# Second-layer weights interleaved high and low, two operands moved to other byte offsets, and one load moved ahead, in a retention, experts and feed-forward kernel

## The chip, the cores and the metric

The kernel runs on one core of one Trainium2 chip. The metric is the time of one execution in microseconds of device time, as the median of several runs; lower is better. One more execution is recorded by the hardware profiler, and all rows below come from it.

## What is computed

Three layers follow each other. The first is a retention layer (8 batches, 8 heads, 576 positions, 64 channels). Its output, 4608 tokens of 512 channels, goes through 8 experts, one of which is chosen for each token. The last layer, which the change is mostly about, is a plain feed-forward layer with a squared ReLU:

```python
def _moe_ref(x, modality_id, w_gate, modality_bias, w1, w2):
    logits = x @ w_gate + modality_bias[modality_id]
    e_idx = np.argmax(logits, axis=1)
    ...
        h = np.maximum(x[mask] @ w1[e], 0.0)
        out[mask] = gate_w[mask, None] * (h @ w2[e])

def _moe2_ref(x, w_in, w_out):        # x 4608x512, w_in 512x2048, w_out 2048x512
    h = np.maximum(x @ w_in, 0.0)
    return (h * h @ w_out).astype(np.float32)
```

## The kernel before

Every product of the experts and of the last layer is made of three TensorE matmuls in the float32r type: each operand is held as a high part and a low part (the rest), and high times high, high times low and low times high are summed in PSUM.

**Experts (`phase12`).** Tokens are sorted by expert into slots "E" and 0 to 8, each of 8 blocks; `us` lists the blocks, numbered i. Blocks 56 to 63 are slot 6 (448 tokens wide), 64 to 71 slot 7 (384 wide), 72 to 79 slot 8 (256 wide). For block i, `first` of block i+1 (12 matmuls, then `hh` on ACT and `hl` on DVE), a transposition of the next slot's tokens where due (`xh` on ACT, `xl` on DVE), and `second` of block i (12 matmuls) are written down in this order. After them come the block's side tasks: splitting the next expert weights (`wx`, `wy`), a portion of the generator `cs`, which converts the last layer's weights (steps L745 to L768, then `cwh` on ACT and `cwl` on DVE, then a store to DRAM as `wc`), and steps of the generator `ex`, which is `combos`. The first step of `combos` first runs all that is left of `cs` (L798), and then issues the load of `eyr`, 1 MB, the first 512 tokens of the last layer's input (L802). Its further steps make the sums and differences that the last layer needs of them (`etx`, `x`).

**Last layer (`phase3`).** It works on 2x2 blocks with 7 products instead of 8, per tile of 512 tokens (9 tiles) and per 256 of the 2048 hidden channels (8 of these, in three passes of 3, 2 and 3, `PASSES`). `one` makes a first-layer product, with weights as the stationary and x as the moving operand; `two` a second-layer product, with h as the stationary and weights as the moving operand. `six` writes the six matmuls of either (L1199 to L1201): stationary high with moving high, stationary high with moving low, stationary low with moving high, twice. All are 128x128 by 256 columns. There are 3024 in the first layer and 3024 in the second. `Plan` sets the order of phase 3: each operation has a cost, what it reads and writes by key, and a due time counted back from TensorE, and the planner lays them out engine by engine. Its loads of weights are `loadw`, at the start of a pass; the loads ahead of the first pass are `wload2` in `phase12`. Loads and stores are issued by SP in the order written.

**Where operands lie.** An address counts bytes within a partition. In the built program before, every x and w tile of the last layer starts at a multiple of 128 (`w000` at 41088, `x0` at 49280, `w100` at 131200), and so do `xh`, `xl`, `hh`, `hl`, `wx` and `wy` of the experts. The three `h` tiles are the exception: they start at 147680, 162016 and 176352, which is 96 above a multiple of 128. All steps inside these tiles are multiples of 512 bytes. The high and low parts of a second-layer weight are two tiles, 8 to 32 KB apart.

Of the kernel before, what the change touches and what calls it, by code (L numbers as in the profile page):

```python
# [25 lines left out]
P = 128  # L26
# [66 lines left out]
def kernel(ctx, tc, qT, kT, kN, vN, modT, w_gate, mbias, w1, w2, w_in, w_out,  # L93
# [318 lines left out]
    def run(gen, n):  # L412
        for _ in range(n):
            if next(gen, 0) == 0:
                return False
        return True
# [298 lines left out]
    def phase12():  # L715
        ring[0] = psG
        with ExitStack() as c1:
# [285 lines left out]
            for i, u in enumerate(us):  # L1003
                s, f = u
                k = seq.index(s)
                nx = seq[k + 1] if k + 1 < len(seq) else None
                if nx is not None and f == (4 if s == "E" else 0):
                    gather(nx)
                if i + 1 < len(us):
                    first(us[i + 1])  # L1010
                if nx is not None:
                    if s == "E" and f == 6:
                        trans(nx, 0)
                        trans(nx, 1)
                    elif s != "E" and 3 <= f <= 6:
                        trans(nx, f - 3)
                if u == (NF, 7):
                    wload2(1, 0, wp)
                if i == 71:
                    tc.mark_branch_hint_location("extra0", 0, HINTED)  # L1020
                second(u)
                if s == "E" and f == 6:
                    trans(nx, 2)
                    trans(nx, 3)
                if i == 2:
                    route_c(last)
                if i == 0:
                    for _ in route_a(last):
                        pass
                    next(cs)  # L1030
                elif i == 1:
                    tb = table()
                    next(tb)
                    for _ in route_b(last, dve):
                        next(tb)
                elif i == 2:
                    ws(6, 2, 7)
                    tab_out()
                    turn = tab_turn()
                    next(turn)  # L1040
                    for _ in range(10):
                        next(tb)
                elif i == 3:
                    while next(tb) != "set":
                        pass
                    turn = chain(turn, tb)
                    ws(8, 2, 11)
                else:
                    wl(i + 9)
                    run(turn, 9)  # L1050
                    fill(wsg(i + 6, 2 if i < 10 else 1, i + 9), part(cs, 2250))
                    if i >= 65:
                        run(ex, 1 if i == 65 else 2)
                    if i == 73:
                        assert next(cs, 0) == 0 and next(ex, 0) == 0
                        extras()
                        wload2(0, 0, cv)
                if u == (NF, 1):
                    wload2(0, 1, wp)
                if u == (NF, 5):  # L1060
                    wload2(0, 2, wp)
                if i == 6:
                    ext = nc.values_load(slots[0:1, 3, 0:1], min_val=0, max_val=NX)
# [3 lines left out]

    def wload2(m, j, pool_, load=True):
        for x in range(2):
            held["w", m, j, x] = pool_.tile([P, 7, 256], F32R, tag="w", name=f"w{m}{j}{x}")  # L1070
            if load:
                sp.dma_start(held["w", m, j, x].bitcast(F32).rearrange("p m c -> p (m c)"), wc[m, PASSES[0][j], x])

# [73 lines left out]
    def phase3():  # L1147
        with ExitStack() as c2:
# [4 lines left out]
                wload2(1, j, wp, False)  # L1153
            WT = [[[held["w", m, j, x] for x in range(2)] for j in range(3)] for m in range(2)]
            XT = [held["x", m] for m in range(7)]
            HT = [sb(f"h{j}", [P, 2, 7, 256]) for j in range(3)]
            ZT = [sb(f"z{j}", [P, 8, 256], F32) for j in range(3)]
            yr = rp.tile([P, KD, TS], F32, tag="raw", name="yr")
            xt = sb("xt", [P, 2, 256], F32)
# [29 lines left out]
            def dma(o, i, kb, r, w, early=False):  # L1189
                plan.add(m_(kb), lambda e: (pool if early else e).dma_start(o, i), r, w, 2.0)  # L1190
# [15 lines left out]
            def loadw(p, m, j0=0):  # L1206
                for j, fp in list(enumerate(PASSES[p]))[j0:]:
                    for x in range(2):
                        dma(WT[m][j][x].bitcast(F32).rearrange("p m c -> p (m c)"), wc[m, fp, x], 917,
                            [], [("w", m, j, x)])  # L1210

# [101 lines left out]
            def two(n, x):  # L1313
# [4 lines left out]
                for q in range(len(PASSES[p])):  # L1318
                    u = HS_[n, q]
                    h, m, w, mo = HT[u % 3], MH[x], WT[1][q], MO[x]  # L1320
                    plan.add(MMS, six([ps[:, 0, :], ps[:, 1, :]],
                                      [((h[:, 0, m, P * b:P * b + P], h[:, 1, m, P * b:P * b + P]),
                                        (w[0][:, mo, :], w[1][:, mo, :])) for b in range(2)],
                                      x in (1, 2, 5) and q == 0),
                             [("h", u % 3, m, 0), ("h", u % 3, m, 1), ("w", 1, q, 0), ("w", 1, q, 1)], [kr])
                v = VO[n]
                oe = OE[v]
                o = {1: oe[:, 0:2, 256:512], 6: oe[:, 0:2, 0:256], 4: oe[:, 2:4, 256:512],
# [101 lines left out]
```

## Time and profile before

| | |
|---|---|
| median of 3 runs | 1345.21 us (1340.93 to 1346.01) |
| the profiled execution: its time | 1348.41 us |
| the profiled execution: span from first to last instruction | 1346.5 us |
| mean granted TensorE clock | 0.995 |
| TensorE (PE) busy | 1312.9 us, 98%, 10639 matmuls |
| weight loads of TensorE (PEld) busy | 1226.4 us, 91% |
| VectorE (DVE), ScalarE (ACT) busy | 76%, 46% |
| DMA, mean over the span | 246 GB/s |
| the last layer on TensorE | from 607.9 to 1338.9 us |

Matmuls are pipelined, so a busy PE says only that it seldom waits: each matmul of the last layer is shown as some 280 ns long, but a new one starts every 117 to 120 ns. What a matmul costs is read from the distance of starts in the order of time.

### The profile page before, as it was taken

The page shows a single profiled execution, that of the slowest core. Times are in us where ns is not written, and L with a number is a line of the kernel's source. Part 1 is how long each engine was busy: PE and PEld are TensorE (multiplying, and loading weights), DVE is VectorE, ACT ScalarE, POOL GpSimd, SP SyncE. Part 2 cuts the span into 40 slices and gives each one's busy share as a digit, 9 for nine tenths or more (in the row PEclk, how much of TensorE's full clock was granted, in tenths as well). Part 3 has the DMA queues.
Part 4 walks back from the last instruction along what each step waited for, and adds up shares of the span by engine and source line. Part 5 has one row for each costly group of instructions (what it writes and reads, how often), then busy time and mean ns, then how long its engine had stood idle before and what let it go on. Part 6 is the DMA issues. An engine that isn't in the chain of part 4 may idle for free.

```text
span 1346.5 us, 26963 instructions
## 1 busy us (share of the span) xinstructions
PE 1312.9 (98%) x10639; PEld 1226.4 (91%) x10639; DVE 1022.8 (76%) x2095; ACT 624.5 (46%) x1283; POOL 125.2 (9%) x170
## 2 busy tenths in 40 slices
PE   7999989999999999999999999999999999999997
PEld 7888877888888889899999999999999999999996
DVE  3787858878787788647788888758788777776665
ACT  1444344454545545536655666534434444433343
POOL 3222112101110110000000000000000011111121
PEclk9999989999999999999999999999999999999999
DMA  9998257788787877887554445668799755655551
GB/s 330 391 351 300 77 189 237 278 279 294 246 299 244 318 263 233 295 330 294 218 208 189 173 172 204 251 257 310 282 342 342 294 203 200 211 174 173 173 188 48
DMA packets 139957, 331.90 MB, mean 246 GB/s; under 512 B 15185, under 2 KB 52849, under 8 KB 139825
## 3 DMA queue, kind: packets, MB, share of 16 engines
q1 hardware_dynamic: 132208, 309.82, 64.3%
q0 software_dynamic: 5840, 19.14, 4.0%
q8 instruction: 85, 1.39, 0.4%
q10 hardware_dynamic: 1776, 1.17, 0.3%
q14 instruction: 48, 0.39, 0.1%
HBM read 222.33 MB, written 107.78 MB: 245 GB/s over the span
## 4 chain that ended last, share of the span: by engine, by line
PE 50%; DVE 4%; ACT 1%; issue 0%; POOL 0%; POOLq 0%; DVEq 0%
PE bank L1201 17%; PE bank L1199 16%; PE bank L1200 16%; DVE z L1177 2%; DVE h L1302 1%; DVE z L1185 1%; ACT h L1301 0%; PE bank L839 0%; PE bank L841 0%; PE bank L840 0%; POOL out L1309 0%; DVE oe L1177 0%; ACT z L1174 0%; DVE x L1177 0%; DVE yr L1177 0%
## 5 line engine op out<-in xcount | busy, mean ns | idle before, releaser
L1199 PE MATMUL bank<-x,w 128*128 128x256 f32 x1008 | 286.0, 284 | 1.5 <-ACT z L1174 1.5
L1200 PE MATMUL bank<-x,w 128*128 128x256 f32 x1008 | 285.7, 283 | 0.5 <-DVE x L1177 0.5
L1199 PE MATMUL bank<-w,h 128*128 128x256 f32 x1008 | 282.8, 281 | 2.4 <-DVE oe L1177 1.6
L1201 PE MATMUL bank<-x,w 128*128 128x256 f32 x1008 | 285.0, 283 | 0.0
L1201 PE MATMUL bank<-w,h 128*128 128x256 f32 x1008 | 282.6, 280 | 1.8 <-DVE h L1302 1.8
L1200 PE MATMUL bank<-w,h 128*128 128x256 f32 x1008 | 282.4, 280 | 1.0 <-DMA w<-wc 1.0
L1174 ACT ACTIVATE z<-bank 128x256 f32<-128x256 f32 x288 | 108.8, 381 | 254.0 <-PE bank L1201 252.0
L1301 ACT ACTIVATE h<-z 128x512 fp32r<-128x512 f32 (+2 forms) x270 | 158.3, 599 | 81.8 <-DVE z L1177 65.1
L1199 PEld LDWEIGHTS bank<-x,w 128*128 128x128 f32 x1008 | 192.5, 191 | 3.1 <-ACT z L1174 3.1
L1200 PEld LDWEIGHTS bank<-x,w 128*128 128x128 f32 x1008 | 192.8, 191 | 1.1 <-DVE x L1177 0.7
L1199 PEld LDWEIGHTS bank<-w,h 128*128 128x128 f32 x1008 | 189.9, 188 | 3.7 <-DVE oe L1177 2.6
L1201 PEld LDWEIGHTS bank<-x,w 128*128 128x128 f32 x1008 | 193.1, 192 | 0.0
L1201 PEld LDWEIGHTS bank<-w,h 128*128 128x128 f32 x1008 | 189.6, 188 | 2.8 <-DVE h L1302 2.7
L1200 PEld LDWEIGHTS bank<-w,h 128*128 128x128 f32 x1008 | 189.5, 188 | 1.2 <-DMA w<-wc 1.2
L1302 DVE TENSOR_TENSOR h<-z,h 128x512 fp32r<-128x512 f32 (+2 forms) x270 | 169.0, 649 | 7.8 <-ACT h L1301 7.8
L1177 DVE TENSOR_TENSOR z<-z,bank 128x256 f32<-128x256 f32 x216 | 89.6, 417 | 69.6 <-PE bank L1201 52.6
L839 PE MATMUL bank<-hh,wy 128*128 128x512 f32 (+3 forms) x320 | 122.5, 383 | 0.0
L839 PE MATMUL bank<-xh,wx 128*128 128x512 f32 (+3 forms) x320 | 119.1, 372 | 1.7 <-DVEq L958 1.7
L840 PE MATMUL bank<-hl,wy 128*128 128x512 f32 (+3 forms) x320 | 119.3, 373 | 0.2 <-DVE hl L856 0.2
L841 PE MATMUL bank<-hh,wy 128*128 128x512 f32 (+3 forms) x320 | 119.2, 373 | 0.0
L841 PE MATMUL bank<-xh,wx 128*128 128x512 f32 (+3 forms) x320 | 118.9, 372 | 0.0
L840 PE MATMUL bank<-xl,wx 128*128 128x512 f32 (+3 forms) x320 | 118.8, 371 | 0.1
(185 smaller groups left out, 2132.5 us busy)
## 6 DMA issues: line engine op xcount, KB each, us to landing
x<-xc SPq DMA_DIRECT2D x112, 512.0 KB
wr<-w SPq DMA_DIRECT2D x80, 512.0 KB
xc<-x SPq DMA_DIRECT2D x63, 512.0 KB
w<-wc SPq DMA_DIRECT2D x32, 896.0 KB
wc<-cwh SPq DMA_DIRECT2D x16, 896.0 KB
wc<-cwl SPq DMA_DIRECT2D x16, 896.0 KB
pd<-oe SPq DMA_DIRECT2D x24, 512.0 KB
xd<-xs SPq DMA_DIRECT2D x9, 1024.0 KB
```

Source lines behind the costliest of these rows:

```text
L839: pe.matmul(ps, lh, rh, start=first, stop=False)
L840: pe.matmul(ps, lh, rl, start=False, stop=False)
L841: pe.matmul(ps, ll, rh, start=False, stop=last)
L1174: plan.add(a_(c), lambda e: e.activation(o, i, f), r, w)
L1177: plan.add(engs or d_(c), lambda e: e.tensor_tensor(out=o, in0=a, in1=b, op=op), r, w)
L1185: e.scalar_tensor_tensor(out=z, in0=z, scalar=0.0, in1=z, op0=ALU.max, op1=ALU.mult)
L1199: e.matmul(ps[n], lh, rh, start=first and n == 0, stop=False, skip_group_check=True)
L1200: e.matmul(ps[n], lh, rl, start=False, stop=False, skip_group_check=True)
L1201: e.matmul(ps[n], ll, rh, start=False, stop=True, skip_group_check=True)
L1301: plan.add(a_(c), lambda e: e.activation(h[:, 0, a:b], z[:, a + 1:b + 1], AF.Copy), rs, ks[0])
L1302: plan.add(d_(c), lambda e: e.tensor_tensor(out=h[:, 1, a:b], in0=z[:, a + 1:b + 1], in1=h[:, 0, a:b].bitcast(F32), op=ALU.subtract), rs + ...
```

## The change

Four edits. (1) A second-layer weight tile holds 4 blocks with high and low side by side (`[P, 4, 2, 256]`): tile 0 blocks 0 to 3, tile 1 blocks 4 to 6. Each is loaded by two DMAs, one for the high and one for the low parts, in rows of 1 KB on the SBUF side, where one DMA of 7 KB rows loaded a tile before. (2) First-layer weight tiles get 32 more elements, and the weights begin 16 elements, 64 bytes, into the tile. (3) The h tiles get 64 more elements, and h begins 56 elements, 224 bytes, into the tile; as the tiles themselves still start 96 above a multiple of 128, h now starts 64 above one (147904, 162496, 177088). (4) The first step of `combos` runs after block 61 and not after block 65; the others stay.

```diff
-                    if i >= 65:
-                        run(ex, 1 if i == 65 else 2)
+                    if i == 61 or i >= 66:
+                        run(ex, 1 if i == 61 else 2)
...
     def wload2(m, j, pool_, load=True):
         for x in range(2):
-            held["w", m, j, x] = pool_.tile([P, 7, 256], F32R, tag="w", name=f"w{m}{j}{x}")
+            if m:
+                held["w", m, j, x] = pool_.tile([P, 4, 2, 256], F32R, tag="w", name=f"w{m}{j}{x}")
+                if load:
+                    for a in range(2):
+                        n = 4 - x
+                        sp.dma_start(held["w", m, j, x][:, 0:n, a, :].bitcast(F32),
+                                     wc[m, PASSES[0][j], a][:, x * 1024:x * 1024 + 256 * n]
+                                     .rearrange("p (m c) -> p m c", c=256))
+                continue
+            wt = pool_.tile([P, 7 * 256 + 32], F32R, tag="w", name=f"w{m}{j}{x}")
+            held["w", m, j, x] = wt[:, 16:16 + 7 * 256].rearrange("p (m c) -> p m c", m=7)
...
-            HT = [sb(f"h{j}", [P, 2, 7, 256]) for j in range(3)]
+            HT = [sb(f"h{j}", [P, 2 * 7 * 256 + 64])[:, 56:56 + 2 * 7 * 256]
+                  .rearrange("p (x m c) -> p x m c", x=2, m=7) for j in range(3)]
...
+                        if m:
+                            n = 4 - x
+                            for a in range(2):
+                                dma(WT[m][j][x][:, 0:n, a, :].bitcast(F32),
+                                    wc[m, fp, a][:, x * 1024:x * 1024 + 256 * n].rearrange("p (m c) -> p m c", c=256),
+                                    131 * n, [], [("w", m, j, x, a)])
+                            continue
...
-                                        (w[0][:, mo, :], w[1][:, mo, :])) for b in range(2)],
+                                        (w[mo // 4][:, mo % 4, 0, :], w[mo // 4][:, mo % 4, 1, :])) for b in range(2)],
...
-                             [("h", u % 3, m, 0), ("h", u % 3, m, 1), ("w", 1, q, 0), ("w", 1, q, 1)], [kr])
+                             [("h", u % 3, m, 0), ("h", u % 3, m, 1)]
+                             + [("w", 1, q, mo // 4, a) for a in range(2)], [kr])
```

On VectorE, at the end of slot 6 of the experts (`hl` 448 wide belongs to block 63, `xl` to the tokens of slot 7):

```order
 L757 TENSOR_TENSOR cwk<-cwk 128x1024
 L759 SCALAR_TENSOR_TENSOR cwk<-craw,cwk 128x1024
+L768 TENSOR_TENSOR cwk<-cwk 128x2x128 x4
+L157 TENSOR_TENSOR cwl<-cwk,cwh 128x768
+L157 TENSOR_TENSOR cwl<-cwk,cwh 128x1024
 L856 SCALAR_TENSOR_TENSOR hl<-bank_90,hh 128x448
 L795 TENSOR_TENSOR xl<-bank_91,xh 128x384
 L157 TENSOR_TENSOR wy<-wr_5558,wy 128x1024
-L768 TENSOR_TENSOR cwk<-cwk 128x2x128 x4
-L157 TENSOR_TENSOR cwl<-cwk,cwh 128x768
 L856 SCALAR_TENSOR_TENSOR hl<-bank_89,hh 128x384
 L157 TENSOR_TENSOR wx<-wr_5604,wx 128x1024
-L157 TENSOR_TENSOR cwl<-cwk,cwh 128x1024
```

The last six steps of the weights' conversion, which were spread over the next two blocks, now stand ahead of block 63's `hl` and of `xl`.

On ScalarE at the same place (`hh` 448 wide and `xh` are the partners of `hl` and `xl` above):

```order
 L156 ACTIVATE wx<-wr_5513 128x1024
+L156 ACTIVATE cwh<-cwk 128x768
+L156 ACTIVATE cwh<-cwk 128x1024
 L855 ACTIVATE hh<-bank_90 128x448
 L794 ACTIVATE xh<-bank_91 128x384
 L156 ACTIVATE wy<-wr_5558 128x1024
-L156 ACTIVATE cwh<-cwk 128x768
 L855 ACTIVATE hh<-bank_89 128x384
```

Both `cwh` copies now stand ahead of `hh` and `xh`.

On SP at the same place (`wr` are expert weights, `wc` the converted weights' stores):

```order
 L439 DMA wr_5648<-w 128x2x512
-L439 ISA
-L439 DMA wr_5688<-w 128x4x256
+L778 DMA wc<-cwh 128x1792
+L778 DMA wc<-cwl 128x1792
+L802 DMA eyr<-yd 128x4x512
+L439 ISA
+L439 DMA wr_5703<-w 128x4x256
```

The last stores of the conversion, which stood behind two of these loads of expert weights, and the load of `eyr`, which stood behind four of them, now stand ahead of them all.

## Rows read from the trace of the kernel before

**Rows 1.** Busy time in two stretches: length, engines, granted clock, DMA share, GB/s.
```profile
210.00:400.00 190.00, 187.57 (x861) 154.49 (x861) 158.38 (x205) 91.80 (x125) 26.04 (x27) 1.00 0.80 277
...
900.00:1000.00 100.00, 100.00 (x845) 100.00 (x845) 79.88 (x173) 41.46 (x91) 0.00 (x0) 1.00 0.82 297
```

**Rows 2.** Matmuls with the weights, from 600 us: duration ns min/median/max, starts.
```profile
L1199 PE MATMUL bank<-x,w x1008: 278/283/387, 607.9 to 1322.9; 128*128 128x256 f32 x168
...
L1201 PE MATMUL bank<-w,h x1008: 276/280/393, 621.8 to 1338.9; 128*128 128x256 f32 x168
```

**Rows 3.** Groups by line from 600 us: busy us, mean ns, idle before.
```profile
L1199 PEld LDWEIGHTS bank<-x,w 128*128 128x128 f32 x1008 | 192.5, 191 | 3.1 <-ACT z L1174 3.1
L1199 PEld LDWEIGHTS bank<-w,h 128*128 128x128 f32 x1008 | 189.9, 188 | 3.7 <-DVE oe L1177 2.6 <-ACT h L1301 0.8 <-ACT oe L1174 0.3
...
L839 PE MATMUL bank<-hh,wy 128*128 128x256 f32 x14 | 4.0, 283 | 0.0
```

**Rows 4.** TensorE in order of time: start us, duration; 29 first-layer matmuls, then 18 second-layer.
```profile
949.76 0.28 PE L1200 MATMUL bank<-x,w 128*128 128x256 f32 x1
...
953.12 0.28 PE L1201 MATMUL bank<-x,w 128*128 128x256 f32 x1
953.25 0.28 PE L1199 MATMUL bank<-w,h 128*128 128x256 f32 x1
...
955.36 0.28 PE L1199 MATMUL bank<-x,w 128*128 128x256 f32 x1
```

**Rows 5.** TensorE in order of time at the end of the experts.
```profile
543.83 0.44 PE L840 MATMUL bank<-xl,wx 128*128 128x384 f32 x1
...
563.61 0.33 PE L839 MATMUL bank<-xh,wx 128*128 128x384 f32 x1
...
565.51 0.34 PE L841 MATMUL bank<-xh,wx 128*128 128x384 f32 x1
568.45 0.69 PE L792 MATMUL bank<-ident,xg 128*128 128x128 f32 x2 [2.60 <-DVE hl L856]
568.79 0.67 PE L839 MATMUL bank<-hh,wy 128*128 128x384 f32 x1
...
571.40 0.34 PE L841 MATMUL bank<-hh,wy 128*128 128x384 f32 x1
```

**Rows 6.** VectorE in order of time there.
```profile
541.55 1.23 DVE L759 SCALAR_TENSOR_TENSOR cwk<-craw,cwk 128x1024 f32<-128x1024 f32 x1
542.69 0.62 DVE L856 SCALAR_TENSOR_TENSOR hl<-bank,hh 128x448 fp32r<-128x448 f32 x1
543.23 0.55 DVE L795 TENSOR_TENSOR xl<-bank,xh 128x384 fp32r<-128x384 f32 x1
...
544.82 1.55 DVE L768 TENSOR_TENSOR cwk<-cwk 128x256 f32<-128x256 f32 x4
546.29 0.95 DVE L157 TENSOR_TENSOR cwl<-cwk,cwh 128x768 fp32r<-128x768 f32 x1
...
565.91 0.69 DVE L809 TENSOR_TENSOR etx<-eyr 128x512 f32<-128x512 f32 x1 [5.88 <-DMA eyr<-yd]
```

**Rows 7.** ScalarE in order of time there.
```profile
539.26 0.55 ACT L855 ACTIVATE hh<-bank 128x448 fp32r<-128x448 f32 x1 [2.66 <-PE bank L841]
539.70 0.49 ACT L794 ACTIVATE xh<-bank 128x384 fp32r<-128x384 f32 x1
...
542.81 0.85 ACT L156 ACTIVATE cwh<-cwk 128x768 fp32r<-128x768 f32 x1 [1.66 <-DVE cwk L759]
...
548.31 1.05 ACT L156 ACTIVATE cwh<-cwk 128x1024 fp32r<-128x1024 f32 x1
```

**Rows 8.** SP's issues in order of time: start, time of issuing.
```profile
556.40 0.55 SPq L802 DMA_DIRECT2D eyr<-yd  x1
...
880.89 2.16 SPq L1190 DMA_DIRECT2D w<-wc  x4
```

**Rows 9.** TensorE's waits from 640 us on: us in total, times, longest.
```profile
PE bank L1200 <- DMA w<-wc: 1.0, 1, 1.0
```

## The prediction

> **What bounds the kernel now.** I looked first at the stretches. In a stretch of the last layer TensorE is busy for all of its 100 us with 845 matmuls at a granted clock of 1.00, while VectorE has 80 and DMA a share of 0.82 [rows 1]. A busy TensorE can still start its matmuls closer together, so the next view is the order of time. There 28 steps between first-layer matmuls take 953.12 - 949.76 = 3.36 us, 120.0 ns each, and 18 second-layer steps 955.36 - 953.25 = 2.11 us, 117.2 ns each [rows 4]. These steps are not waits: no row between them names a releaser. With 3024 matmuls in each layer (3 x 1008 [rows 2]) they make 362.9 + 354.4 = 717 us, more than half of the span. TensorE's pace in the last layer is what bounds that layer; what an edit does to a wait there is small beside what it does to a step.
>
> A step has a part that the clock explains. At 2.4 GHz (granted clock 1.00) 256 columns take 106.7 ns. 13.3 ns are left in the first layer and 10.5 in the second. What the reader is to see is that this rest differs between two streams of the same shape, and that the same difference stands in the durations: 283 against 280 ns at the median of a matmul [rows 2], 191 against 188 for a weight load [rows 3]. It is not the layer as such: the experts' matmuls of the same 256 columns last 283 ns [rows 3], like the first layer's. In the built program the experts' operands and the first layer's start at multiples of 128 bytes, stationary and moving alike; only the second layer's stationary, h, starts 96 above one. So of three groups the two with equal starts are slow and the one with unequal starts is faster. That is a correlation over three groups, not a proof.
>
> **Edits 2 and 3, first-layer weights and h at 64 bytes.** They make both layers' stationary operand start 64 above a multiple of 128, with the moving operand on one. No row shows a start of 64, so the price is bounded. The nearest row for the first layer is the second's 117.2: a gain of 2.8 x 3024 = 8.5 us. The best that any row shows is a shortest matmul of 276 ns [rows 2]. As 3 ns less duration went with 2.8 ns less step, 276 stands for a step of 120 - 7 = 113 ns; both layers there would gain (7.0 + 4.2) x 3024 = 33.9 us. On the other side, 64 could act as 0 does: then the second layer goes from 117.2 to 120.0 and loses 8.5 us. I take the middle of 117.2 and 113, which is 115, for both layers, because 64 lies farther from both neighbouring multiples of 128 than 96 does. That is a choice. It gives 5.0 x 3024 = 15.1 us in the first layer and 2.2 x 3024 = 6.7 us in the second, **-21.8 us**.
>
> Against it stands a rule of the Trainium skill (TensorE: Matmul & The Clock Gate, Part 2, the step-by-step section and the one on the back-to-back gap): TensorE reads the moving operand and the next weights through two independent ports, so that loading weights takes nothing from the running matmul, and the gap is columns / 2.4 + 2.5 ns. By that rule both layers would step at 109.2 ns now, and a byte offset would be worth 0. The rows have 120.0 and 117.2, so the second half of the rule does not hold here, and what the first half says is the first rival below.
>
> **Edit 1, high and low side by side.** The matmuls keep number, order and shape; only the moving address changes, from tiles 8 to 32 KB apart to blocks 1 KB apart. The first layer's x has its two parts in one tile already and is the slower one [rows 4], so I give this 0 for the step. What it costs is in the loads: pieces of 1 KB where there were 7 KB. The stretch with mostly small pieces (expert weights in rows of 1 and 2 KB) moves 277 GB/s at a share of 0.80, 346 at a full share; the stretch of the last layer, mostly 4 KB, 297 at 0.82, 362 [rows 1]. So small pieces are some 5% dearer. The place where it can be seen is a change of pass: at 880.89 SP issues four loads of these weights, 3.67 MB, in 2.16 us [rows 8], and TensorE waits 1.0 us for one of them, once [rows 9]. 5% of 3.67 MB at 362 GB/s (10.1 us) is 0.5 us. Issuing eight instead of four costs SP 2.16 us more, and the loads of x behind them start that much later. Against it, the first second-layer product then needs two loads of 0.52 MB and not two of 0.92. Bounds: 1.0 us gained (the wait gone) and 2.7 us lost (0.5 + 2.2, all on the path). I take **+0.5 us**, nearer to nothing since the transfer itself decides, not its issue.
>
> **Edit 4, the load of `eyr` after block 61.** First what it removes. `eyr` is issued at 556.40 [rows 8], and VectorE stands from 560.0 to 565.91 for it [rows 6]. Behind that wait in VectorE's queue is an `hl`, and TensorE waits for it: from 565.51 the next start is at 568.45, where a step of this shape is (565.51 - 563.61) / 11 = 0.17 us [rows 5]. That is 2.8 us. After it the steps are longer: eight take 571.40 - 568.79 = 2.61 us where 8 x 0.17 = 1.4 would do, 1.2 us more. The matmuls there last 0.67 us at first against 0.33 before, what the lower of the two clock levels, 1.2 GHz, would make of them. Together 4.0 us, which the earlier load should save.
>
> Now what it adds. The first step of `combos` also runs the rest of the conversion, and the order shows six VectorE and two ScalarE instructions ahead of block 63's `hh`, `xh`, `hl` and `xl`. On VectorE L759 frees the queue at 542.69, four L768 follow (1.55) to 544.24 [rows 6]. On ScalarE `cwh` of 768 runs at 542.81 as before; `cwh` of 1024 needs the L768 and takes 1.05, to 545.3 [rows 7]; then `hh` and `xh`, which ran at 539.26 and 539.70 [rows 7], end at about 545.8 and 546.2. On VectorE `cwl` of 768 (0.95) ends at 545.1, `cwl` of 1024 (1.23, as L759 of the same shape) starts after its `cwh` at 545.3 and ends at 546.6, `hl` (0.62) at 547.1, `xl` (0.55, overlapping by 0.1) at 547.6 [rows 6]. TensorE's matmul with this `xl` ran at 543.83 [rows 5] and would now start at 547.6: 3.8 us later. So the wait moves from one place to another. If the clock falls there too, 1.2 us come on top. Stores and `eyr` (2.9 MB) then stand ahead of an expert weight load on SP; at 346 GB/s that is 8 us of transfer from 546.6, so `eyr` lands about 555, well before its use at 560, and the expert weights behind it about 557; with TensorE itself 3.8 us later by then I count nothing for them. Bounds: 4.0 gained (the wait hidden by something that I overlook), 1.0 lost. I take -4.0 + 3.8 + half of the 1.2, **+0.4 us**.
>
> **Sum.** -21.8 + 0.5 + 0.4 = -20.9 us. The profiled execution took 1348.4, so 1327.5; the runs' median is 3.2 below it, so **1324 us**.
>
> **Rivals.**
> (A) The offset does nothing: steps stay at 120.0 and 117.2, and h at 96 was faster for another reason (its place far from the other tiles, or that ScalarE and VectorE write it). Then 1345.2 + 0.9 = 1346. For it: only three groups. Against: durations within one layer vary, from 276 or 278 to their medians [rows 2], at one and the same start.
> (B) Starts repeat every 64 bytes: 64 is then equal to 0, and 96, which is 32, was the better place. The first layer stays, the second goes to 120.0: +8.5 + 0.9, 1354.6, slower. It decides once the second layer's steps pass 119.1 (1.9 x 3024 = 5.8 us, with the 0.9 half a per cent of the time) and the first does not gain. For it: both slow groups lie at 0 of either period. Against: nothing in the rows.
> (C) One step only: the first layer comes to 117.2, the second stays: -8.5 + 0.9, 1337.6.
> (D) Both come to the shortest seen, 113: -33.9 + 0.9, 1312. For it: single matmuls do so now. VectorE would then be at about 84% in the stretch [rows 1], not the bound.
>
> **How the numbers follow.** A measurement of this kernel can tell about 0.5%, 6.7 us, from no change. I give the forecast 0.34 (1318 to 1331), D 0.18, C 0.15, A 0.17, B 0.14, and 0.02 that loads at the changes of pass cost more than the bound. Faster: 0.34 + 0.18 + 0.09 of C, which lies at the edge, 0.61. Same: 0.17 + 0.06, 0.23. Slower: 0.16. The range leaves out B and the lowest part of D: 1304 to 1350.
>
> **What would show it.** The distance of starts in the last layer's rows: 115 in both layers (forecast), 117 and 117 (C), 120 and 120 (B), 120 and 117 (A), 113 (D); weight loads near 186 where the steps are short. At the end of the experts: no wait of VectorE for `eyr`, no TensorE wait of 2.8 us near 565, but one of some 4 us near 544, ended by `xl`. At the changes of pass: a wait for `w` of 0 to 2.7 us. I am wrong if the steps do not move together with the start of the stationary operand, or if the conversion's last steps do not hold up block 64's first product.

## The result and the profile after

The changed kernel takes 1325.28 us (median of 6 runs, 1322.11 to 1336.03) against 1343.65 us before (6 runs on the same chip, 1340.93 to 1346.01): a ratio of 0.9886, 95% interval 0.9852 to 0.9919. Forecast were 1324 us and faster. The runs of after spread over 14 us, those of before over 5; two of the six lie at 1335 and 1336, the other four between 1322 and 1326. The profiled execution of after is the slowest, 1336.03 us with a span of 1334.2, so its rows show less of the gain than the median does; that of before, 1348.41 us, is 4.8 above the median too.

First the windows of after; columns as in [rows 1].

```profile
210.00:400.00 190.00, 187.50 (x861) 154.46 (x860) 158.20 (x204) 91.01 (x124) 25.95 (x27) 1.00 0.80 278
...
545.00:553.00 8.00, 6.51 (x19) 5.73 (x20) 3.56 (x5) 4.04 (x9) 0.00 (x0) 0.57 0.95 335
...
565.00:573.00 8.00, 8.00 (x49) 7.93 (x48) 7.48 (x13) 4.62 (x9) 0.00 (x0) 1.00 0.72 259
...
900.00:1000.00 100.00, 100.00 (x852) 100.00 (x851) 81.91 (x177) 41.79 (x92) 0.00 (x0) 1.00 0.86 308
1060.00:1300.00 240.00, 240.00 (x2040) 240.00 (x2040) 174.20 (x371) 103.88 (x242) 32.54 (x60) 1.00 0.57 200
```

The experts' stretch is as it was. In the last layer the same 100 us hold 852 matmuls and not 845 [rows 1], with TensorE busy throughout in both: the steps are shorter. At the end of the experts, 545 to 553 us, stands a new hole with a granted clock of 0.57, which is most of it at the lower level, 1.2 GHz; the hole that [rows 5] shows from 565 on is gone.

Now TensorE in order of time, with the rows that answer to [rows 5] first and those that answer to [rows 4] behind them.

```profile
542.31 0.34 PE L841 MATMUL bank<-xh,wx 128*128 128x384 f32 x1
545.48 0.44 PE L839 MATMUL bank<-xh,wx 128*128 128x384 f32 x1 [2.84 <-ACT xh L794]
546.93 0.69 PE L840 MATMUL bank<-xl,wx 128*128 128x384 f32 x1 [1.01 <-DVE xl L795]
547.41 0.52 PE L841 MATMUL bank<-xh,wx 128*128 128x384 f32 x1
547.73 0.58 PE L839 MATMUL bank<-hh,wy 128*128 128x448 f32 x1
...
551.84 0.57 PE L841 MATMUL bank<-hh,wy 128*128 128x448 f32 x1
...
689.91 0.28 PE L1212 MATMUL bank<-w,h 128*128 128x256 f32 x1
...
693.08 0.28 PE L1210 MATMUL bank<-x,w 128*128 128x256 f32 x1
693.69 0.38 PE L1211 MATMUL bank<-x,w 128*128 128x256 f32 x1 [0.34 <-DVE x L1188]
...
940.24 0.28 PE L1210 MATMUL bank<-x,w 128*128 128x256 f32 x1
...
943.54 0.28 PE L1211 MATMUL bank<-x,w 128*128 128x256 f32 x1
```

From 689.91 to 693.08 lie 28 steps of both layers: 3.17 us, 113.2 ns each. From 940.24 to 943.54 lie 28 first-layer steps: 3.30 us, 117.9 ns each. Both are shorter than the first layer's 120.0 of [rows 4], and the two layers now step alike; but there are two levels, 113.3 and 117.8. Read over the whole trace, a level holds from one wait of TensorE to the next, often over many waits: 113.3 from 634 to 884 us, 117.8 from 888 us to nearly the end. The change came at a wait of 2.3 us for `x` at 887.84 (below). Means over the profiled run are 116.2 in the first layer and 116.1 in the second.

The weight loads of after, duration in ns as minimum/median/maximum:

```profile
L1210 PEld LDWEIGHTS bank<-x,w x1008: 186/188/193, 609.1 to 1310.8; 128*128 128x128 f32 x168
L1211 PEld LDWEIGHTS bank<-x,w x1008: 187/188/193, 609.2 to 1310.9; 128*128 128x128 f32 x168
L1212 PEld LDWEIGHTS bank<-x,w x1008: 186/192/193, 609.4 to 1311.0; 128*128 128x128 f32 x168
```

The first layer's 191 of [rows 3] is 188 for two lines of the three. The third, the load of the low half, has 192 at the median: at the 117.8 level one load in three is long, at 113.3 none is.

TensorE's waits of after from 640 us on (us in total, times, longest), which answer to [rows 9]:

```profile
PE bank L1211 <- DVE x L1188: 3.2, 7, 1.1
PE bank L1210 <- DMA x<-xc: 2.3, 1, 2.3
...
PE bank L1212 <- DMA w<-wc: 0.9, 1, 0.9
```

The wait of 1.0 for `w` has become one of 0.9, and one of 2.3 for `x` stands behind it. SP's rows fit that: in after the second-layer loads of that change of pass are eight, whose row spans 6.30 us, where that of four spans 2.16 [rows 8], and the loads of `x` stand behind them. Of the 6.30 us, 1.1 are SP waiting for TensorE after the second load; the eight issues themselves take 4.8.

```profile
872.35 6.30 SPq L1201 DMA_DIRECT2D w<-wc  x8
878.77 17.47 SPq L1201 DMA_DIRECT2D x<-xc  x8
```

### The profile page after: what moved, and what is told of

Read it like the earlier page. It is cut to its first block, busy times and chain, and to the rows that moved or that the text cites. A ratio compares the mean times of both kernels' runs of the same rounds, so it can differ in the third digit from the quotient of the medians.

```text
span 1334.2 us, 26978 instructions
## 1 busy us (share of the span) xinstructions
PE 1294.7 (97%) x10639; PEld 1209.6 (91%) x10639; DVE 1021.8 (77%) x2095; ACT 624.4 (47%) x1283; POOL 125.3 (9%) x170
## 4 chain that ended last, share of the span: by engine, by line
PE 43%; DVE 10%; DMA 1%; issue 1%; POOL 0%; POOLq 0%; DVEq 0%
PE bank L1211 14%; PE bank L1210 14%; PE bank L1212 14%; DVE z L1188 4%; DVE h L1320 3%; DVE z L1196 1%; DVE x L1188 1%; DVE yr L1188 1%; DMA w<-wc 1%; DMA x<-xc 1%; PE bank L839 0%; PE bank L840 0%; PE bank L841 0%; POOL out L1327 0%; DVE oe L1188 0%
## 5 line engine op out<-in xcount | busy, mean ns | idle before, releaser
L1211 PE MATMUL bank<-x,w 128*128 128x256 f32 x1008 | 282.5, 280 | 4.2 <-DVE x L1188 4.2
L1210 PE MATMUL bank<-x,w 128*128 128x256 f32 x1008 | 281.9, 280 | 2.3 <-DMA x<-xc 2.3
L1212 PE MATMUL bank<-x,w 128*128 128x256 f32 x1008 | 281.8, 280 | 0.9 <-DMA w<-wc 0.9
L1211 PEld LDWEIGHTS bank<-x,w 128*128 128x128 f32 x1008 | 189.3, 188 | 5.8 <-DVE x L1188 5.8
L1212 PEld LDWEIGHTS bank<-x,w 128*128 128x128 f32 x1008 | 191.9, 190 | 1.1 <-DMA w<-wc 1.1
L1210 PEld LDWEIGHTS bank<-x,w 128*128 128x128 f32 x1008 | 189.4, 188 | 2.6 <-DMA x<-xc 2.5
```

Source lines behind the costliest of these rows:

```text
L1210: e.matmul(ps[n], lh, rh, start=first and n == 0, stop=False, skip_group_check=True)
L1211: e.matmul(ps[n], lh, rl, start=False, stop=False, skip_group_check=True)
L1212: e.matmul(ps[n], ll, rh, start=False, stop=True, skip_group_check=True)
```

## Experiments

### The change in three parts

Each part alone in the kernel before, and the two edits of data without that of the load, all on one chip. There the kernel before took 1344.07 us (21 runs, 1342.12 to 1347.73).

**Starts alone** (first-layer weights and h):

```diff
-            held["w", m, j, x] = pool_.tile([P, 7, 256], F32R, ...)
+                wt = pool_.tile([P, 7 * 256 + 32], F32R, ...)
+                held["w", m, j, x] = wt[:, 16:16 + 7 * 256]...
-            HT = [sb(f"h{j}", [P, 2, 7, 256]) for j in range(3)]
+            HT = [sb(f"h{j}", [P, 2 * 7 * 256 + 64])[:, 56:56 + 2 * 7 * 256]...
```

> Edits 2 and 3 alone (first-layer weights and h start 64 bytes above a multiple of 128; high and low second-layer weights stay in two tiles, the load stays after block 65). Theory 1, the start of the stationary operand sets the step: both layers step at 113.3 or 117.8 ns, as in the changed kernel, and the time is 12 to 30 us below that of before. Theory 2, the neighbourhood of high and low weights does it: steps stay at 120 and 117.4 and the time within 5 us of before.

Measured: 1323.27 us (4 runs, 1321.73 to 1333.7), ratio 0.9869 (0.9825 to 0.9913). Its window in the last layer:

```profile
1060.00:1300.00 240.00, 240.00 (x2120) 240.00 (x2119) 183.26 (x392) 110.78 (x262) 34.72 (x64) 1.00 0.56 199
```

2120 matmuls where after's profiled run has 2040: 113.2 ns for each against 117.6. Its steps have a mean of 114.0 in both layers, 117.8 only in three stretches of 20 to 45 us. The last layer takes 707.5 us against 731.0. That adds up: some 5780 steps within a layer, each 4.6 ns shorter, are 26.6 us; TensorE's waits between them (steps over 130 ns, beyond the mean) grew from 13.8 to 17.8 us, which gives 4.0 back, and the steps from one layer to the other gave the 0.9 that is left. These are two single traces, so their 23.5 us need not be the 20.8 between the medians: the execution of before that was traced is itself 4 to 5 us above its medians. One such wait stands in after's rows at 693.69: at the short step TensorE comes to the next `x` before VectorE has it ready.

**Side by side alone:**

```diff
-            held["w", m, j, x] = pool_.tile([P, 7, 256], ...)
+                held["w", m, j, x] = pool_.tile([P, 4, 2, 256], ...)
```

> Edit 1 alone (high and low second-layer weights side by side, loaded in 1 KB rows; all starts and the load as before). Theory 1: first layer 120.0, second 117.4 ns, time within 4 us of before. Theory 2: the second layer falls to 113 to 118 ns on average under 117, and the time by 5 us or more; the first layer stays at 120.0.

Measured: 1342.47 us (10 runs), ratio 0.9988 (0.9978 to 0.9998): 1.6 us less. The steps are 119.8 and 117.4 as before, so nothing came of the address itself. The wait of 1.0 for `w` is gone, one of 1.6 for `x` is new, and among the small waits of the last layer those for `h` and `z` are shorter, that for VectorE's `x` longer; where the 1.6 us are was not settled.

**The load alone:**

```diff
-                    if i >= 65:
-                        run(ex, 1 if i == 65 else 2)
+                    if i == 61 or i >= 66:
+                        run(ex, 1 if i == 61 else 2)
```

> Edit 4 alone (first step of combos after block 61). By my sum: the wait near 565 goes (4.0 us), one of 3.8 us near 543 comes, with 1.2 us more if the clock falls: -0.2 to +1.0 us. From the profile of the changed kernel, where the waits there are 3.2 and 1.4 us and 13 steps are of the low clock: +2.5 us. Rival, the load is worth its distance: -4 us.

Measured: 1346.41 us (10 runs), ratio 1.0019 (1.0009 to 1.0029): 2.3 to 2.5 us more. The same two waits as in after stand in TensorE's queue, 2.7 for `xh` and 1.0 for `xl`, and the 2.6 for `hl` is gone.

**Starts and side by side, without the load edit:** after with the old two lines in place of the load's.

> Edits 1 to 3, with the load left after block 65. Steps as in the changed kernel, 113.3 or 117.8 ns by stretches. If edit 4 costs 2.5 us, this is 2 to 3 us faster than the changed kernel in the same state of the steps, some 1320; if edit 4 gains, it is 4 us slower, some 1329.

Measured: 1327.36 us (6 runs, 1320.53 to 1337.02), ratio 0.9885 (0.9842 to 0.9927). That can't be told from after or from the starts alone. The profiled run, 1329.99 us, steps at 113.4 up to 1047 us and at 117.8 from there on. Three profiled runs with these starts, on two chips where before takes 1344, order themselves by their mean step: 114.0 ns and 1322.88 us, 115.3 and 1329.99, 116.2 and 1336.03. 2.1 ns over 5780 steps are 12 us, most of the 13 between first and last; the last also has the load edit's loss, and the short steps give some back in waits.

### What the start does to a step, by itself

TensorE alone, groups of 120 matmuls at different starts, six of each pair. Each of the two runs of this kind is one execution; the granted clock is 1.00 in all groups.

> The computation is left out; TensorE only takes groups of 120 matmuls of 128x128 by 128x256 in triples of the kernel's form (high by high, high by low, low by high), 6 groups for each of 12 pairs of starts (stationary, moving, each modulo 128 bytes): a (0,0) b (16,0) c (32,0) d (48,0) e (64,0) f (80,0) g (96,0) h (112,0) i (64,64) j (0,64) k (32,32) l (96,64). Theory (what counts is that the two operands start at different places modulo 128): a, i and k take 120.0 ns a step, e and j as little as each other, 113.3 to 117.8, and g and l sit between, with 117.4 for g. Rival 1 (only the stationary's own start counts): i is as quick as e, j as slow as a at 120.0. Rival 2 (a period of 64 bytes): e and a are alike. Of the two levels 113.3 and 117.8 that the kernel after the change shows from wait to wait: if the matmul of the triple before which the wait stands picks the level, the groups of one pair differ by that place; if the length of the wait picks it, by one or three reads; if neither, they differ without order or not at all.

A row of the order of time is one group: start, length, operands, number of matmuls, and the wait ahead of it.

```profile
543.26 14.50 PE L48 MATMUL main<-ma,sa 128*128 128x256 f32 x120 [0.52 <-DVE tmp L51]
...
575.29 14.46 PE L48 MATMUL main<-ma,sc 128*128 128x256 f32 x120 [1.43 <-DVE tmp L51]
...
607.07 13.89 PE L48 MATMUL main<-ma,se 128*128 128x256 f32 x120 [1.43 <-DVE tmp L51]
622.39 14.27 PE L48 MATMUL main<-ma,sf 128*128 128x256 f32 x120 [1.43 <-DVE tmp L51]
...
669.66 14.51 PE L48 MATMUL main<-mi,si 128*128 128x256 f32 x120 [1.44 <-DVE tmp L51]
685.60 14.40 PE L48 MATMUL main<-mi,sj 128*128 128x256 f32 x120 [1.44 <-DVE tmp L51]
701.44 14.51 PE L48 MATMUL main<-mk,sk 128*128 128x256 f32 x120 [1.44 <-DVE tmp L51]
717.39 14.46 PE L48 MATMUL main<-mi,sl 128*128 128x256 f32 x120 [1.44 <-DVE tmp L51]
...
984.80 14.17 PE L48 MATMUL main<-ma,se 128*128 128x256 f32 x118 [1.19 <-DVE tmp L51]
...
1062.68 13.66 PE L48 MATMUL main<-mi,sj 128*128 128x256 f32 x118 [1.20 <-DVE tmp L51]
```

`sa`, `si` and `sk` have equal starts (0, 64 and 32 on both sides): 14.5 us, 118.7 ns a step, whichever the common start is (one group of `sa` had 120.0). `se` (stationary 64, moving 0) and `sj` (0 and 64) are each other's mirror: 13.89 us (113.3 ns) in one group of `se`, 14.40 (117.8) in the one of `sj`, and the other way round in the later rows, 14.17 and 13.66 for 118. `sl` (96 and 64) has a difference of 32, and in all six groups it steps at 118.3 like `sc` (32 and 0), not like 96 with 0. So here it is the difference of the starts that counts and not the stationary's place, and 64 has two levels here too, with no kernel around it. The two rivals on the start fall. The levels came without order: `se` was at 113.3 in one group of six, `sj` in three, over both lengths of the wait and all three places of it. The other differences: 80 gave 116.7 in all six groups (14.27 us), 112 gave 117.4, 48 gave 118.1, 32 gave 118.3; 16 gave 116.7 or 120.0, and 96 gave 117.4, 118.7 or 120.0.

The second run of this kind asks whether a start near 64, or another order in the triple, keeps to the short level.

> As the first run of steps alone (the computation is left out), all moving operands at 0 modulo 128 bytes. a (64), b (56), c (60), d (68), e (72), f (76), g (4), h (8): the stationary's start with the kernel's triple (high by high, high by low, low by high). i to l: start 64 with other triples: i high by high, low by high, high by low; j low by high, high by high, high by low; k high by high, high by low, high by high; l high by high, low by low, high by low. Theory (the step goes by the difference of the starts, with 64 as the low point of what was tried, and each wait leaves a group of steps in one of two phases): a shows both 113.3 and 117.8 again, 60 and 68 lie between that and the 116.7 of 80, and the order within the triple, which only changes which weights are loaded, does not take the slower level away. Rival 1 (starts not divisible by 16 bytes cost more): b to f at 118 or above. Rival 2 (the slower level comes of the change from the high to the low weights in a triple): k, which has the high weights alone, shows one level, 113.3.

```profile
541.06 13.89 PE L49 MATMUL main<-mv,sa 128*128 128x256 f32 x120 [0.52 <-DVE tmp L52]
...
572.22 14.60 PE L49 MATMUL main<-mv,sc 128*128 128x256 f32 x120 [1.44 <-DVE tmp L52]
588.26 14.40 PE L49 MATMUL main<-mv,sd 128*128 128x256 f32 x120 [1.43 <-DVE tmp L52]
...
620.00 14.66 PE L49 MATMUL main<-mv,sf 128*128 128x256 f32 x120 [1.44 <-DVE tmp L52]
...
699.00 14.40 PE L49 MATMUL main<-mv,sk 128*128 128x256 f32 x120 [1.43 <-DVE tmp L52]
...
887.42 13.78 PE L49 MATMUL main<-mv,sk 128*128 128x256 f32 x119 [1.32 <-DVE tmp L52]
```

64 is a point, not the middle of a trough: 60 (`sc`) takes 119.4 ns, 68 (`sd`) 117.8, 76 (`sf`) 120.0, and none of the seven others tried is under 117.8. There the theory failed, and the first rival was nearer. The order within the triple takes neither level away: each of the five orders at 64 shows both, with one to five groups of six at 113.3. With that the second rival falls too: `sk`, with the high weights alone, shows both levels, 14.40 us for 120 and 13.78 for 119.

### Two tests of that in the kernel

**A start of 80 in place of 64**, which by itself gave one level:

```diff
+                held["w", m, j, x] = wt[:, 20:20 + 7 * 256]...
+            HT = [sb(f"h{j}", [P, 2 * 7 * 256 + 64])[:, 60:60 + 2 * 7 * 256]...
```

> The kernel before with the first-layer weights and the h buffers at 80 bytes modulo 128 in place of 64. In the run of steps alone a start of 80 gave 116.7 ns in all six groups, where 64 gave 113.3 or 117.8. Theory (the two levels of 64 are what spreads the runs of the kernel after the change over 14 us): here every stretch steps at 116.7 in both layers, the runs lie within 5 us of each other, and the time is 1335 (about 5800 steps by 1.9 ns are 11 us, of which the 64-byte run kept four fifths). Rival (what spreads them is something else, a transfer or the clock): the spread is 10 us or more here too.

Measured: 1348.9 us (11 runs, 1348.22 to 1350.8) against 1347.35 for before on that chip (21 runs), ratio 1.0016 (1.0007 to 1.0025). No gain: in the kernel 80 steps at 118.7 or, from 842 to 1015 us, at 120.0, 119.0 on average in both layers. The first layer gained 0.8 ns and the second lost 1.6. So 116.7 did not carry over from the groups alone to the kernel, where the operands lie at other addresses. The spread is 2.6 us, as the theory has it, but that says little, since its two levels differ by 1.3 ns and not by 4.5.

**The experts' stationary weights at 64:**

```diff
-            x = new(wp, [P, 2, KD, 2 * P], F32R, "w", "wx")
+            x = new(wp, [P, 2080], F32R, "w", "wx")[:, 16:2064]...
```

> The kernel before with one edit elsewhere: the experts' stationary weights, all at 0 modulo 128 bytes with their moving operands at 0 too, go to 64 bytes. Theory (the difference of starts sets the step of any such matmul that loads new weights, at any width): the steps of 226.7 ns (512 columns), 173.3 (384) and 120.0 (256) fall by 2.2 to 6.7 ns, over 1920 matmuls 4 to 13 us, and the time by most of it, 1332 to 1340. Rival 1 (with 512 columns the weight load is long over and nothing is to be had): only the 256-wide steps fall, under 1 us in all. Rival 2 (the experts' stage waits for its weights to be split): steps fall, waits of TensorE take their place, and the time stays.

Measured: 1350.28 us (10 runs), ratio 1.0021 (1.0012 to 1.0031), slower by 2.9. A window in the experts' 512-wide part, before:

```profile
250.00:450.00 200.00, 200.00 (x920) 165.47 (x919) 163.97 (x205) 98.44 (x134) 24.69 (x25) 1.00 0.80 274
```

and with the edit, with a group of 256 columns from the groups by line behind it:

```profile
250.00:450.00 200.00, 200.00 (x905) 162.85 (x905) 160.83 (x200) 96.37 (x131) 24.09 (x25) 1.00 0.78 269
```

```profile
L839 PE MATMUL bank<-hh,wy 128*128 128x256 f32 x32 | 8.9, 277 | 0.0
```

At 256 columns the edit does what it does in the last layer: 277 ns against the 283 of [rows 3], and steps of 114 to 115 against 120. At 512 columns the edit's starts are the worse of the two: 905 matmuls in 200 us and not 920, steps of 231.6 against 227 to 228, while at 384 nothing moves. TensorE has no new wait (4.9 us for `hl` against 5.0). Some 1300 matmuls of 512 columns lose 4.2 ns (5.5 us), 190 of 256 columns gain 5.4 (1.0), 190 of 448 gain 2.5 (0.5): 4 us lost. The last layer gives about 1 us back in this trace: its steps go from 119.8 and 117.4 to 119.0 and 117.9 on average. That comes near the 2.9 that show. Its starts modulo 128 have not changed, and five other traces with these starts have 119.8 and 117.4; but the edit makes the experts' tiles 128 bytes longer, and in the built program the h tiles of the last layer lie 1280 bytes higher and most of its weight tiles 128 to 1152, all multiples of 128. So the starts modulo 128 may not be all that counts. The theory "at any width" is wrong; rival 1 had the 256-wide steps right and missed the loss, rival 2 falls. Of the two starts, which is the better depends on the width.

### The load without the drain

The first step of `combos` is split: the tile and the load of the sums come first, and the conversion is drained where it was before.

```diff
             def combos():
+                yr = cv.tile([P, KD, TS], F32, tag="w", name="eyr")
+                sp.dma_start(yr, yd[:, 0:TS].rearrange("(c p) t -> p c t", p=P))
+                yield 1
                 for _ in cs:
                     pass
...
-                    if i >= 65:
-                        run(ex, 1 if i == 65 else 2)
+                    if i == 62 or i >= 65:
+                        run(ex, 1 if i <= 65 else 2)
```

> The kernel before with one edit: the load of the sums is issued after block 62 in place of 65, and nothing else of that turn is moved, so that no drain of the conversion comes with it. Theory (what costs in the change's own edit is the draining of the conversion, not the earlier load): VectorE's 5.9 us wait for the sums is gone, TensorE's wait of 2.8 us near 565 us and its 1.2 us at the lower clock too, nothing comes in their place at 542 to 548, and the time is 4 us less, 1340. Rival (the queue): the expert weights that stand behind the load in SP's queue come later by as much, TensorE waits for them, and the time stays within 1 us or grows.

Measured: 1341.37 us (10 runs) against 1343.74 (19 runs), ratio 0.9978 (0.9968 to 0.9987): 2.4 us less. TensorE's waits from 500 to 606 us are only these:

```profile
PE bank L840 <- DVEq L959: 1.4, 1, 1.4
PE bank L841 <- DVE hl L857: 0.2, 1, 0.2
```

The 2.6 us for `hl` of [rows 5] is gone, VectorE's 5.9 for `eyr` too, and from 545 to 553 and from 565 to 573 us the clock is 1.00 with TensorE busy for all of both. The mechanism is as expected; of the 4 us the runs show 2.4, for a reason that stands with the load's term below.

> As the run with block 62, one block earlier: the load stands where the change puts it, but without the drain. Theory: 4 us less than before, as with block 62, since the load of either has landed when VectorE comes to it; against the change's own edit alone (2.5 us more than before) that leaves 6.5 us to the drain. Rival (the queue): one block earlier pushes one more transfer of expert weights back, and the time is over that of block 62 by a wait of TensorE of 1 us or more.

Measured, one block earlier: 1341.25 us (10 runs), ratio 0.9985 (0.9975 to 0.9995), the same within the intervals. So the place of the load costs nothing. Issued after block 61 without the drain it gives 2.5 us, with it it takes 2.3 to 2.5: about 5 us are the drain's.

### All together, beside the changed kernel

> The changed kernel with its load edit replaced: the load of the sums goes after block 62 and nothing of the conversion is drained for it; the 64-byte starts and the weights side by side stay. Sum of the parts as measured alone: 1323.3 of 1344.1 for the starts (-20.8), -1.6 for side by side, -2.4 for the undrained load: 24.8 us less than before, ratio 0.9815, and about 4.9 us less than the kernel after the change on the same chip, where the drained load alone gave +2.5. Rival (the parts hide behind each other, since the shorter steps uncover waits for transfers): no better than the kernel after, ratio 0.986 or more.

> The changed kernel as it is, on the same chip as the version with the undrained load, to compare the two. Theory (two levels of the step at 64 bytes, one of which each wait leaves by chance): its runs spread over 10 us or more, where those of the kernel before on this chip lie within 6 us, and the profiled run's time goes with the share of its steps at 117.8 against 113.3. Rival (the spread of the first timing was the chip's): runs within 6 us as before.

On this chip the kernel before took 1349.51 us (11 runs, 1347.15 to 1351.07). The version with the undrained load took 1332.28 (4 runs, 1330.85 to 1334.52), ratio 0.9879 (0.9865 to 0.9893); the changed kernel as it is 1339.47 (6 runs, 1338.35 to 1342.68), ratio 0.9930 (0.9917 to 0.9942). The ranges don't meet: without the drain it is 7.2 us better, where 4.9 were expected, and it beats both kernels. The two profiled runs are 11.4 us apart; 5.8 of that lie at the end of the experts, where the drain is, and about 5 in the mean step of the last layer (below), which goes by the mix of levels and not by the drain. How much of the 7.2 between the medians is of that kind is not shown. Against before the undrained version gives 17.2 and not 24.8, so the parts do not add up fully. By the profiled runs, its mean step of 114.9, in place of 114.0 with the starts alone, is 5 us of the 7.6 that are missing, and waits within a layer of 19.8 us in place of 17.8 are 2. TensorE at the end of the experts, with the undrained load:

```profile
545.00:553.00 8.00, 8.00 (x46) 7.88 (x45) 6.51 (x10) 5.38 (x8) 0.00 (x0) 1.00 0.65 238
...
1060.00:1300.00 240.00, 233.72 (x2013) 231.94 (x2013) 172.22 (x368) 101.95 (x240) 34.84 (x64) 1.00 0.56 193
```

No hole from 545 to 553, where the changed kernel has a clock of 0.57. In the last layer stand 6.3 us without a matmul in 240, where the first profile of after has none; the largest of its waits from 610 us on are these:

```profile
PE bank L1211 <- ACT z L1186: 5.8, 7, 1.1
PE bank L1211 <- DMA x<-xc: 2.8, 3, 2.2
PE bank L1212 <- DVE x L1189: 2.6, 5, 1.0
```

The changed kernel has 5.5 us of the wait for `z` on this chip, where its first profile and the run without the load edit show 0.2 or less. Both kernels changed level at many of their waits here, and the mean steps are 114.9 for the version with the undrained load and 115.8 for the changed kernel. That also answers the second expectation: the spread of the changed kernel's runs is 4.3 us and not 10. The rival was right on the spread. The two levels are there in the trace, but they change so often here that their mix may well average out within a run; that reading is not tested.

## Why the prediction was right, and where it was off

**The time and the largest term hold.** Forecast were -21.8 us for the starts of 64, measured -20.8 (12 to 24 less by the interval); the reason given, that the two operands' starts make the step, is shown by the mirrored pair, by the three equal pairs and by the two pairs 32 apart of the run of steps alone. Rival A (the start does nothing) and rival B (a period of 64 bytes) fall with the same rows, C with two equal layers. D, 113 in both layers, came half true: it is one of two levels. The choice of 115 stands for a mixture that I did not foresee: 113.3 and 117.8, with means of 114.0 to 116.2 from one profiled run to another. So the mechanism was right, and that the size came so near is luck in part.

**The way from step to time was simplified.** All of a step's gain was counted as time. The run with the starts alone shows 26.6 us of shorter steps and 4.0 us of new waits. In that trace the term comes out near the forecast because the mean step was below 115, and the waits took this back.

**The correlation was read too widely.** "Two groups with equal starts are slow, one with unequal starts is faster" holds for 256 columns. Among the 512-wide matmuls the equal starts are the better ones, and a start of 80 brought nothing in the kernel. The argument that 64 lies farthest from both neighbouring multiples of 128 was a lucky one, as 60 and 68 show.

**Side by side:** +0.5 forecast, -1.6 measured (0.3 to 3 by the interval). The cost on SP is there, 4.8 us for the eight issues where 4.3 were worked out, and it shows as the wait for `x`. By the trace, less waiting elsewhere outweighs it; which wait makes the 1.6 us was not settled.

**The load is the term that was mis-sized:** +0.4 forecast, 2.3 to 2.5 measured. What was removed was right: VectorE starts `etx` at 565.65 in after without a wait (last row below), against 565.91 after 5.88 us in [rows 6], and the window from 565 to 573 has a clock of 1.00. The new wait was right in place and cause, the drained conversion ahead of block 64's first product. VectorE of after there, in order of time:

```profile
541.97 1.56 DVE L768 TENSOR_TENSOR cwk<-cwk 128x256 f32<-128x256 f32 x4
543.45 0.95 DVE L157 TENSOR_TENSOR cwl<-cwk,cwh 128x768 fp32r<-128x768 f32 x1
544.65 1.23 DVE L157 TENSOR_TENSOR cwl<-cwk,cwh 128x1024 fp32r<-128x1024 f32 x1 [0.26 <-ACT cwh L156]
545.79 0.62 DVE L856 SCALAR_TENSOR_TENSOR hl<-bank,hh 128x448 fp32r<-128x448 f32 x1
546.33 0.55 DVE L795 TENSOR_TENSOR xl<-bank,xh 128x384 fp32r<-128x384 f32 x1
...
565.65 0.68 DVE L809 TENSOR_TENSOR etx<-eyr 128x512 f32<-128x512 f32 x1
```

`xl` ends at 546.9, worked out was 547.6. TensorE loses 3.0 us from 542.31 to 545.48 and 1.3 to 546.93, beyond a step of 0.18 each: 4.3, near the 3.8. Worked out was one wait ended by `xl`; the larger part is ended by `xh`, which stands behind the two `cwh` on ScalarE. What was wrong is the price of the clock, of which I took half of 1.2 us behind the new wait and the whole 1.2 behind the old one. In after the steps from 547.73 to 551.84 are 11 in 4.11 us, 374 ns each, where a 448-wide step takes 204 elsewhere in the trace: 1.9 us there and 0.8 in the five steps next to them, which are long too. That is 2.7. In the trace of the load alone only six steps are that long, and the loss is 1.5 us:

```profile
545.00:553.00 8.00, 6.50 (x26) 5.90 (x27) 3.62 (x6) 5.00 (x9) 0.00 (x0) 0.79 0.95 336
```

So the clock's price differs from trace to trace, and behind the old wait it does so too. The same window in two traces with the load after block 65, before first and side by side alone second:

```profile
565.00:573.00 8.00, 5.40 (x25) 5.08 (x25) 7.04 (x12) 6.48 (x12) 0.00 (x0) 0.79 0.55 203
565.00:573.00 8.00, 5.93 (x36) 5.46 (x35) 7.70 (x13) 6.96 (x14) 0.00 (x0) 1.00 0.66 235
```

In side by side alone, the starts alone and the run with 80 the clock stays at 1.00 there, and the wait for `hl` is 2.0 to 2.1 us; in before, the run without the load edit and that of the experts' weights the wait is 2.5 to 2.6 and the clock falls. The 4.0 us of the forecast were read in a trace of the dearer kind. From the first matmul of block 64's first product to the first of the last layer the traces have 66.1 and 66.4 us with the load after block 65 where the clock fell (the experts' run, with steps of its own, left out), 64.4 to 64.5 where it stayed, 67.0 to 68.3 with the drained load and 61.7 to 61.9 with the undrained one. So by these traces the change's edit costs 0.7 to 4.0 us, the undrained load gains 2.4 to 4.6, and 5.1 to 6.6 between the two are the drain's. The medians, 2.3 to 2.5 us lost and 2.4 gained, lie inside these ranges, the gain at the low end.

The Trainium skill (TensorE: Matmul & The Clock Gate, Part 2, on the two ports) says that loading the next weights takes no read bandwidth from the running matmul. No run here measures that, as every matmul loads new weights; what the runs show is a step that depends on the starts of both operands, 113.3 to 120.0 ns at equal width and clock, and never 109.2. The formula behind the 109.2 of the prediction is given in the same part's section on the back-to-back gap for an isolated matmul; of a stream of weight loads and matmuls, as here, that section says that both set the distance. So by that section the 109.2 was not to be expected here.

**Open.** What picks the level at a wait (neither its place in the triple nor its length did); what counts besides the starts modulo 128, another part of the address or the kernel's other work, since equal pairs took 118.7 ns alone and 119.8 in the first layer of before, and the last layer's steps moved by 0.5 to 0.8 ns in the experts' run; why 80 does not carry over; why the waits for `z` are there on one chip only. The place of the stationary operand by width, beyond 64 for the experts, was not searched.

## What to carry to other kernels

When TensorE is busy all the time and its steps are longer than the columns and the clock explain, compare streams of the same shape: here 5 ns a step, set by where the two operands start in a partition, were worth 21 us, for two slices of a tile. Test each width in its own kernel, because of the two starts tried there the better for 256 columns was the worse for 512, and what groups alone showed for 80 did not carry over. And when a load is moved ahead, look at what its step in the program drains with it: the same load cost 2.3 us with the drain and gained 2.4 without it.

## What the runs showed of the hardware

- Of a 128x128 by 128x256 matmul with new weights each time, at a clock of 1.00, the step goes by the difference of the operands' starts modulo 128 bytes where TensorE runs alone: 113.3 or 117.8 ns at 64, 116.7 at 80, 118.3 at 32, 118.7 or 120.0 at 0, and 117.8 to 120.0 at 60, 68 and 76. In the kernel something counts besides, as 80 gave 118.7 or 120.0 there.
- One pair of starts can have two or three levels. A level is kept between waits, over up to 2246 steps in the profile of after, and changes only at one.
- At 512 columns the order is the other way: 227 to 228 ns at equal starts, 231.6 with 64 between them.
- The clock behind a wait differed between traces with the same TensorE work at the end of the experts: 0.79 over 8 us with 25 matmuls after a wait of 2.6 us (before), 1.00 with 36 after one of 2.1 (side by side alone).
